# Long convolution and MLP on one core: three channel groups, k loaded without PE transposes, a spectral table built on chip, and listed priorities

## The chip, the cores and the metric

The kernel runs on one core of a Trainium2 chip. The core has five engines, each with an instruction stream that it works through in order: PE (matmuls; its weight loads are shown apart as PEld), DVE (vector), ACT (scalar), POOL (GpSimd) and SP (here it only issues transfers). They are tied together by semaphores. The metric is device time in microseconds, lower is better. The kernel before takes 258.33 us (median of 4 runs, 258.3 to 258.42).

## The reference

The sequence length is S = 2048, the width D = 640, the hidden width F = 1728, all in bf16. With `ln` a layer norm without weights:

```
k_shift[s, d] = sum over t of k_pad[s + t, d] * shift_k[d, 3 - t]     # 4 taps, 3 rows of zeros in front
kv            = k_shift * v
y             = causal convolution over s of kv[:, d] with ssm_k[d, :] (by FFT of length 2 * S) + kv * ssm_D
h             = q + ln(q) * y
out           = h + mish(ln(h) @ w1 + b1) @ w2
```

## The kernel before, in words

The convolution is an FFT written as matmuls. Position s is split as 16 * t1 + t2 (t1 = 0..127, t2 = 0..15). The 640 channels lie in 5 blocks of 128 (`dc`), each of 32 groups of 4 channels, so that there are 160 such groups (`dg`). The stages, by the names in the code:

- `k1` (L485): PE transposes of the loaded `ssm_k` block, 16 per block, evicted from PSUM in two halves (`k1ev`).
- `s1k` and `s1v` (`stage1`, L428 and L429): the DFT over t1, one matmul pair per `dg`. Eight groups make one PSUM tile of 128x1024 f32, and there are 4 tiles per block; each is evicted by `ev` (L317 on ACT, L319 on DVE).
- `s2k` and `s2v` (`s2_pe`, L457): twiddle and DFT over t2. For each of 128 frequencies f a 128x128 block of the table `G` is the stationary operand, and the `nd` channel groups of one group list are the moving one. The lists are `GRP_DC`: blocks 0 to 2 (`nd` 96) and blocks 3 and 4 (`nd` 64). `s2_chunks` packs frequencies into PSUM tiles: 13 chunks of 10 frequencies (960 elements; the last smaller), and 8 of 16 (1024 elements). `s2k` is evicted by `kpev` into `KP`, `s2v` by `xev` (ACT only) into a ring `xa` of 4 slots.
- `swap` (L583): 20 transfers from SBUF to SBUF copy `KP` with its partition halves exchanged into `KPS`. `KPS` lies where `ssm_k` and part of `k` were.
- `ktpe`, `ktev` (L510): k is loaded with t1 on the partitions (L396), and each of its 5 blocks is transposed by 16 PE transposes and evicted in two halves.
- `ks` (L533): the 4-tap shift as matmuls on 32-row tiles of the array, 76 per block, with a part of transposed k as the stationary operand and diagonal taps as the moving one. `kv` (L544, DVE) multiplies by v.
- `prod` (L659, DVE): for each chunk x times `KP` and x times `KPS`, in place.
- `i1` (L670, L671): inverse DFT over g, evicted by `i1ev` into `zb`. `i2` (L712): the last inverse stage per t2.
- Then for each t2: `lnx` (L719), `wb` (L724), `h` (L728), layer norm (L733, L734, POOL), `dr` (L742), transposes (L749); and the MLP in six units of tokens, `m1` (L768), `mish` (L774), `m2` (L784), residual (L793), output.

The order is not that of the code. Each operation is registered with `OP` or `DMA`: its engines and estimated durations, its dependences, its buffer slots and a number `prio`. `_schedule` (L96) is a list scheduler over these estimates: among the operations that can start within 0.3 us of the earliest one, it takes the lowest `prio`. The instructions are then emitted in order of planned start, so that every engine and the SP queue get a fixed order, and on the chip each waits for the head of its own queue. All transfers but those at the start of ACT's and POOL's streams are on SP's queue, and the planner takes them for one serial resource.

Most SBUF is one arena with offsets given by hand. `zb` takes the place of the `bks` and `bvs` buffers of its group, `w1` that of `G`, `w2` that of `KPS`.

Of the kernel before, what the change touches and what calls it, by code (L numbers as in the profile page):

```python
# [10 lines left out]
ALU = mybir.AluOpType  # L11
# [4 lines left out]
S = 2048  # L16
# [10 lines left out]
GRP_DC = [[0, 1, 2], [3, 4]]  # L27
GRP_DG = [(0, 96), (96, 160)]
# [3 lines left out]
OFF_KN = 40960  # L32
OFF_K = 61440
OFF_G = 81920
OFF_BA = 114688
OFF_BB = 139264
OFF_V = 155648
OFF_KK = 176128
OFF_KT = 184320
OFF_KVB = 192640  # L40
OFF_KVB2 = OFF_KK
OFF_XA = OFF_KT
OFF_END = 204928
# [7 lines left out]
OFF_HC = OFF_KT  # L51
OFF_OB = OFF_KT + 3840

# [39 lines left out]
_SEM = 0.18  # L93

# [102 lines left out]
def _make_tables():  # L197
    bf = ml_dtypes.bfloat16
    t1 = np.arange(128, dtype=np.float64)
    f1 = np.arange(128, dtype=np.float64)  # L200
    t2 = np.arange(16, dtype=np.float64)
    g = np.arange(16, dtype=np.float64)
    T = {}
    phi = 2 * np.pi * (f1[None, :] + 0.5) * t1[:, None] / 256
    fcfs = np.stack([np.cos(phi), -np.sin(phi)], axis=1).reshape(128, 256)
    psi = 2 * np.pi * (f1[None, :, None] + 0.5 + 256 * g[None, None, :]) * t2[:, None, None] / 4096
    c, s = np.cos(psi), np.sin(psi)
    R0 = np.zeros((2, 16, 128, 2, 16))
    R0[0, :, :, 0, :] = c
    R0[1, :, :, 0, :] = s  # L210
    R0[0, :, :, 1, :] = -s
    R0[1, :, :, 1, :] = c
    G = np.zeros((2, 2, 16, 2, 128, 2, 4, 16))
    for dp in range(2):
        for dm in range(2):
            G[:, dp, :, dm, :, :, 2 * dp + dm, :] = R0
    T["G"] = G.reshape(128, 128 * 128).astype(np.float32).astype(bf)
    th = 2 * np.pi * g[:, None] * t2[None, :] / 16
    cg, sg = np.cos(th), np.sin(th)
    A1 = np.zeros((2, 4, 16, 2, 16, 4))  # L220
    A2 = np.zeros((2, 4, 16, 2, 16, 4))
    for dl in range(4):
        A1[0, dl, :, 0, :, dl] = cg
        A1[1, dl, :, 0, :, dl] = -cg
        A1[0, dl, :, 1, :, dl] = sg
        A1[1, dl, :, 1, :, dl] = -sg
        A2[0, dl, :, 0, :, dl] = -sg
        A2[1, dl, :, 0, :, dl] = -sg
        A2[0, dl, :, 1, :, dl] = cg
        A2[1, dl, :, 1, :, dl] = cg  # L230
    theta = 2 * np.pi * (f1[:, None, None] + 0.5) * (16 * t1[None, None, :] + t2[None, :, None]) / 4096
    T["t2m"] = np.stack([np.cos(theta) / 2048, -np.sin(theta) / 2048], axis=2).reshape(128, 4096).astype(np.float32).astype(bf)
    consts = np.concatenate([np.eye(128), fcfs, np.tile(np.eye(32), (4, 1)), A1.reshape(128, 128), A2.reshape(128, 128)], axis=1)
    T["consts"] = consts.astype(np.float32).astype(bf)
    return T
# [3 lines left out]
def kernel(  # L239
# [88 lines left out]
    a12_b = consts[:, 416:672].rearrange("p (a f) -> p a f", a=2)  # L328
    mhalf = small.tile([P, 16], F32, name="mhalf")
# [28 lines left out]
    OP("d_consts", ("act", 0.8), w=["consts", "Drow"], emit=emit_consts, prio=-2, lat=3.0)  # L358
# [26 lines left out]

    kn_t = lambda: big("kn", [P, NDC, S], OFF_KN)
    for dc in range(NDC):
        DMA(f"d_kn{dc}", 524e3, (lambda e, dc=dc: nc.sync.dma_start(kn_t()[:, dc, :], A_ssm_k[dc * P:(dc + 1) * P, :])),
            w=[("kn", dc)], prio=1 + dc * 0.01)
    G_t = lambda: big("G", [P, P, P], OFF_G)  # L390
    k_t = lambda: big("k", [P, 16, D], OFF_K)
    v_t = lambda: big("v", [P, 16, D], OFF_V)
    kview = A_k.rearrange("b (p a) d -> p (b a) d", a=16)
    vview = A_v.rearrange("b (p a) d -> p (b a) d", a=16)
    for h in range(2):
        DMA(f"d_k{h}", 1.31e6, (lambda e, h=h: nc.sync.dma_start(k_t()[:, h * 8:(h + 1) * 8, :], kview[:, h * 8:(h + 1) * 8, :])),  # L396
            w=[("k", h)], prio=1.1 + 0.01 * h)
    for c in range(4):
        DMA(f"d_G{c}", 1.05e6, (lambda e, c=c: nc.sync.dma_start(G_t()[:, c * 32:(c + 1) * 32, :].rearrange("p f q -> p (f q)"),
                                                                dram["G"][:, c * 4096:(c + 1) * 4096])),  # L400
            w=[("G", c)], prio=1.2 + 0.01 * c)
# [8 lines left out]
    R_KT = ring("kt", 2)  # L410
# [7 lines left out]
    def stage1(prefix, dc, get_src, src_rt, bname, get_dst, dg_base, prio):  # L418
        for gi in range(4):
# [10 lines left out]
            OP(f"{prefix}pe{dc}_{gi}", ("pe", 0.44), r=["consts"], allocs=[rt], uses=[src_rt], emit=pe, prio=prio,  # L430
# [14 lines left out]
    def s2_pe(prefix, grp, ci, get_src, bname, prio, xa=None, after=()):  # L445
# [4 lines left out]
        def pe(e):  # L450
# [4 lines left out]
            for fl in range(nf):  # L455
# [4 lines left out]
               r=keys + [("G", c) for c in range(f0 // 32, (f0 + nf - 1) // 32 + 1)],  # L460
# [3 lines left out]
    def ps2_views(rt, nd, per, nf):  # L464
        if nf <= per:
            return [(rt.tile[:, 0:nf * nd].rearrange("p (f g) -> p g f", f=nf), 0, nf)]
        if nf == 2 * per:
            return [(rt.tile.rearrange("p (b x) -> p b x", b=2)[:, :, 0:per * nd].rearrange("p b (f g) -> p g b f", f=per), 0, nf)]
        return None

    B_t = [lambda n: big(n + "A", [P, P, 96], OFF_BA), lambda n: big(n + "B", [P, P, 64], OFF_BB)]
# [3 lines left out]
    def kernel_dc(dc, grp):  # L475
# [10 lines left out]
        o1 = OP(f"k1pe{dc}", ("pe", 1.0), r=[("kn", dc), "consts"], allocs=[rt, kk], emit=pe, prio=10)  # L486
# [12 lines left out]
    KT = {}  # L499

    def shift_t(dc, prio):
        rt = _RT(PS, f"kt_{dc}")
        kt = _RT(R_KT, f"kt{dc}")

        def pe(e):
            slot(R_KT, kt, "kT", [P, 16, P + 2], OFF_KT, 4160)
            nc.gpsimd.memset(kt.tile[:, :, 0:2], 0.0)
            pt = ps_alloc(rt, BF16).rearrange("p (t d) -> p t d", t=16)
            for t2 in range(16):
                nc.tensor.transpose(pt[:, t2, :], k_t()[:, t2, dc * P:(dc + 1) * P], ident_b)  # L510
        o1 = OP(f"ktpe{dc}", ("pe", 0.95), r=[("k", 0), ("k", 1), "consts"], allocs=[rt, kt], emit=pe, prio=prio)
        wr = []
        for h in range(2):
            def evf(e, h=h):
                ev(e, kt.tile[:, h * 8:(h + 1) * 8, 2:P + 2], rt.tile.rearrange("p (t d) -> p t d", t=16)[:, h * 8:(h + 1) * 8])
            wr.append(OP(f"ktev{dc}_{h}", EV2(1024), uses=[rt, kt], emit=evf,
                         prio=prio, after=[o1] + wr))
        KT[dc] = (kt, wr)

    def shift_s(dc, prio):  # L520
        kt, wr = KT[dc]
# [3 lines left out]
        def ks(e):  # L525
            kvb.tile = view([P, 64, 16, 2], OFF_KVB + dc * 4096 if dc < 3 else OFF_KVB2 + (dc - 3) * 4096)
            outs = [ps_alloc(x).rearrange("p (i t d) -> p i t d", i=2, t=16) for x in rts]
            for src in range(-3, 16):
                j0, j1 = max(0, -src), min(4, 16 - src)
                for i in range(4):  # L530
                    rows = slice(32 * i, 32 * i + 32)
                    lhs = kt.tile[rows, src, 2:P + 2] if src >= 0 else kt.tile[rows, src + 16, 1:P + 1]
                    nc.tensor.matmul(outs[i // 2][:, i % 2, src + j0:src + j1, :], lhs, diagm[rows, dc * 4 + j0:dc * 4 + j1, :],  # L533
                                     start=(src == -3), stop=(src == 15), skip_group_check=True)
        o2 = OP(f"kspe{dc}", ("pe", 1.3), r=["diagm"], allocs=rts + [kvb], uses=[kt], emit=ks, prio=prio,
                after=wr + ([o for o in ops if o.name.startswith("s1kpe")] if dc >= 3 else []))
# [13 lines left out]
    for grp in range(2):  # L550
        for dc in GRP_DC[grp]:
            kernel_dc(dc, grp)
    for dc in range(NDC):
        shift_t(dc, 10.5 + 0.01 * dc)
    for dc in range(NDC):
        shift_s(dc, 11.5 + 0.01 * dc)
    for grp in range(2):
        nd, per, ch = s2_chunks(grp)
        for ci in range(len(ch)):
# [16 lines left out]
            OP(f"kpev{grp}_{ci}", EV(nf * nd), w=[("KP", grp, ci)], uses=[rt], emit=evf, prio=11, after=[o])  # L576
    def swap(grp):
        nd, per, ch = s2_chunks(grp)
        for half in range(2):
            for g0 in range(GRP_DG[grp][0], GRP_DG[grp][1], 16):  # L580
# [4 lines left out]
                free = ("k1pe",) + (("ktpe",) if g0 >= 80 else ())  # L585
# [4 lines left out]
    swap(0)  # L590
    GRP_BVS = {}
    for grp in range(2):
# [9 lines left out]
    swap(1)  # L602
# [26 lines left out]
    zb_t = [lambda: big("zbA", [P, 2, 16, 384], OFF_BA), lambda: big("zbB", [P, 2, 16, 256], OFF_BB)]  # L629

    for grp in range(2):
# [3 lines left out]
        for ci in range(len(ch)):  # L635
            xa = _RT(R_XA, f"xa{grp}_{ci}")
            free = [x for x in ops if x.name.startswith("kspe")] if ci == 0 else []
# [17 lines left out]
            def f2(e, xa=xa, f0=f0, nf=nf, nd=nd, d0=d0, d1=d1):  # L655
                x = xa.tile[:, 0:nf * nd].rearrange("p (g f) -> p g f", f=nf)
                for tt in (KP_t(), KPS_t()):
                    kp = tt[:, d0:d1, f0:f0 + nf]
# [43 lines left out]
    for t2 in range(16):  # L702
# [5 lines left out]
        def pe(e, t2=t2, rt=rt):  # L708
            py = ps_alloc(rt)
            for grp, (c0, n) in enumerate(((0, 384), (512, 256))):  # L710
                for ri in range(2):
                    nc.tensor.matmul(py[:, c0:c0 + n], t2m_t()[:, t2, ri, :], zb_t[grp]()[:, ri, t2, :], start=(ri == 0), stop=(ri == 1))  # L712
        o_pe = OP(f"i2pe{t2}", ("pe", 0.57), r=["t2m"] + [("zb", 0, gi) for gi in range(12)] + [("zb", 1, gi) for gi in range(8)],
                  allocs=[rt], emit=pe, prio=pr)
# [7 lines left out]
        def wbf(e, rt=rt, lnx=lnx):  # L722
            for (c0, n, d0) in ((0, 384, 0), (512, 256, 384)):
                nc.vector.tensor_tensor(lnx.tile[:, d0:d0 + n], rt.tile[:, c0:c0 + n], lnx.tile[:, d0:d0 + n], ALU.mult)  # L724
# [74 lines left out]

    order = _schedule(ops)  # L800
# [38 lines left out]
```

## Time and profile before

| what | value |
|---|---|
| median of 4 runs | 258.33 us (258.3 to 258.42) |
| the profiled execution | 258.35 us |
| its span, first to last instruction | 256.5 us |
| what lies around the span | 1.85 us |
| PE busy | 227.2 us (89%) |
| DVE busy | 151.2 us (59%) |
| ACT busy | 143.5 us (56%) |
| mean granted PE clock | 0.953 |
| HBM read, written | 20.33 MB, 2.62 MB |

"Busy" is the time in which an engine's instructions run. A row of the profile names line, engine, operation, what is written and read, the shape and the count. "Idle before" is the time for which an engine had nothing running before an instruction, with the instruction that ended the wait. A duration in a row is that of one instruction; neighbours overlap, so where a sum needs the pace of an engine, the distance from start to start in the timeline is used.

### The profile page before, as it was taken

How to read it: one execution, taken by the hardware profiler on the slowest of the kernel's cores; microseconds unless marked ns; L12 is line 12 of the kernel's file. 1: busy time of each engine (PE TensorE's matmuls, PEld its weight loads, DVE VectorE, ACT ScalarE, POOL GpSimd, SP SyncE). 2: the span in 40 equal slices, each digit the busy share in tenths (PEclk: the TensorE clock that was granted, in tenths of full speed). 3: DMA queues.
4: the chain of work that ended last, by engine and by line, in shares of the span. 5: the costliest groups of instructions: out<-in, count | busy, mean ns of one | idle time of the engine just before them, and what ended most of it. 6: DMA issues, size and time to landing. Idle time of an engine off the chain costs nothing.

```text
span 256.5 us, 6925 instructions
## 1 busy us (share of the span) xinstructions
PE 227.2 (89%) x3039; PEld 171.3 (67%) x3039; DVE 151.2 (59%) x297; ACT 143.5 (56%) x196; POOL 22.6 (9%) x56
## 2 busy tenths in 40 slices
PE   8798779848957899849899999999999999999993
PEld 4797778738846799829878746645776467644772
DVE  0778789983799988089798898609912002200121
ACT  2687876616978699957958654565211630066100
POOL 5000000000000000212221223102200000000000
PEclk9999999997995599986999999999999999999999
DMA  6999925999960277300000000000011001000001
GB/s 237 328 419 417 421 100 128 223 221 216 352 270 3 46 301 220 130 0 1 3 0 29 27 3 0 34 20 1 9 45 51 0 3 51 27 28 0 26 28 51
DMA packets 8913, 28.65 MB, mean 112 GB/s; under 512 B 1009, under 2 KB 4914, under 8 KB 7474
## 3 DMA queue, kind: packets, MB, share of 16 engines
q1 hardware_dynamic: 8624, 28.02, 33.0%
q8 instruction: 24, 0.39, 0.6%
q10 hardware_dynamic: 146, 0.17, 0.4%
q0 software_dynamic: 112, 0.01, 0.1%
q14 instruction: 7, 0.06, 0.1%
HBM read 20.33 MB, written 2.62 MB: 90 GB/s over the span
## 4 chain that ended last, share of the span: by engine, by line
PE 64%; DVE 18%; ACT 8%; issue 5%; DMA 3%; SPq 0%; DVEq 0%; ACTq 0%
PE banks L784 24%; PE banks L768 22%; DVE arena L319 6%; DVE arena L659 6%; ACT arena L317 5%; PE banks L428 3%; DMA arena<-in_A_ssm_k_dram 3%; PE banks L671 3%; PE banks L670 2%; DVE arena L544 2%; PE banks L457 2%; PE banks L749 2%; ACT arena L719 2%; PE banks L533 1%; ACT arena L774 1%
## 5 line engine op out<-in xcount | busy, mean ns | idle before, releaser
L317 ACT CAST arena<-banks 128x1024 bf16<-128x1024 f32 (+2 forms) x77 | 72.0, 1008 | 21.1 <-PE banks L429 13.1
L774 ACT ACTIVATE arena<-banks,b1s 128x512 bf16<-128x512 f32 (+2 forms) x84 | 44.3, 545 | 45.1 <-PE banks L768 44.0
L768 PE MATMUL banks<-arena 128*128 128x512 bf16 (+2 forms) x420 | 65.9, 317 | 1.4 <-ACT arena L317 0.8
L784 PE MATMUL banks<-arena 128*128 128x320 bf16 x448 | 62.3, 299 | 0.0
L784 PEld LDWEIGHTS <-arena 128*128 128x128 bf16 x448 | 43.7, 98 | 17.5
L768 PEld LDWEIGHTS <-arena 128*128 128x128 bf16 x420 | 37.5, 103 | 25.3 <-issue 1.7
L793 DVE TENSOR_TENSOR arena<-banks,arena 128x640 bf16<-128x640 f32 x16 | 13.1, 817 | 60.2 <-PE banks L784 60.1
L319 DVE CAST arena<-banks 128x1024 bf16<-128x1024 f32 (+3 forms) x27 | 30.4, 1161 | 10.9 <-PE banks L429 7.1
L457 PE MATMUL banks<-arena 128*128 128x96 bf16 (+1 forms) x512 | 25.0, 210 | 6.8 <-ACT arena L317 3.7
L428 PE MATMUL banks<-consts,arena 128*64 128x128 bf16 x320 | 23.0, 229 | 7.2 <-issue 3.6
L457 PEld LDWEIGHTS <-arena 128*128 128x128 bf16 x512 | 22.7, 105 | 8.8 <-issue 8.3
L317 ACT COPY arena<-banks 128x640 bf16<-128x640 bf16 (+1 forms) x17 | 13.5, 806 | 25.6 <-PE banks L749 18.7
L659 DVE TENSOR_TENSOR arena<-arena 128x960 bf16<-128x960 bf16 (+2 forms) x42 | 24.5, 666 | 0.8 <-ACT arena L317 0.8
L429 PE MATMUL banks<-consts,arena 128*64 128x128 bf16 x320 | 23.4, 230 | 0.0
L429 PEld LDWEIGHTS <-arena 128*64 128x64 bf16 x320 | 20.1, 116 | 4.9 <-issue 4.8
L428 PEld LDWEIGHTS <-arena 128*64 128x64 bf16 x320 | 20.4, 116 | 4.4 <-issue 3.8
L670 PE MATMUL banks<-consts,arena 128*128 128x128 bf16 x160 | 20.1, 228 | 2.3 <-DVE arena L659 2.1
L724 DVE TENSOR_TENSOR arena<-banks,arena 128x384 bf16<-128x384 f32 (+1 forms) x32 | 13.7, 471 | 12.4 <-PE banks L712 7.3
L671 PE MATMUL banks<-consts,arena 128*128 128x128 bf16 x160 | 20.0, 228 | 0.2 <-DVE arena L659 0.2
L670 PEld LDWEIGHTS <-arena 128*128 128x128 bf16 x160 | 16.4, 102 | 2.2 <-DVE arena L659 2.2
L671 PEld LDWEIGHTS <-arena 128*128 128x128 bf16 x160 | 16.4, 103 | 0.8 <-DVE arena L659 0.4
L719 ACT ACTIVATE arena<-arena,nmr,r1v 128x640 bf16<-128x640 bf16 x16 | 14.1, 926 | 1.1 <-DVE arena L728 1.1
(46 smaller groups left out, 168.2 us busy)
## 6 DMA issues: line engine op xcount, KB each, us to landing
arena<-arena SPq DMA_DIRECT2D x20, 256.0 KB, 6.2
arena<-tab_G SPq DMA_DIRECT2D x4, 1024.0 KB, 20.6
arena<-in_A_ssm_k_dram SPq DMA_DIRECT2D x5, 512.0 KB, 6.4
arena<-in_A_k_dram SPq DMA_DIRECT2D x2, 1280.0 KB, 13.8
arena<-in_A_v_dram SPq DMA_DIRECT2D x2, 1280.0 KB, 22.9
arena<-in_A_q_dram SPq DMA_DIRECT2D x2, 1280.0 KB, 9.1
out_dram<-arena SPq DMA_DIRECT2D x16, 160.0 KB, 1.8
arena<-in_B_w_dram SPq DMA_DIRECT2D x1, 2160.0 KB, 8.2
```

Source lines behind the costliest of these rows:

```text
L317: nc.scalar.copy(o, i)
L319: nc.vector.tensor_copy(o, i)
L428: nc.tensor.matmul(ps1[0:64, gl, :], lhs, fcfs_b[:, 0, :], start=True, stop=True)
L429: nc.tensor.matmul(ps1[64:128, gl, :], lhs, fcfs_b[:, 1, :], start=True, stop=True)
L457: nc.tensor.matmul(ps2[:, c0:c0 + nd], G_t()[:, f0 + fl, :], src[:, f0 + fl, :], start=True, stop=True)
L659: nc.vector.tensor_tensor(kp, x, kp, ALU.mult)
L670: nc.tensor.matmul(pz[:, gl, :], KP_t()[:, dg, :], a12_b[:, 0, :], start=True, stop=False)
L671: nc.tensor.matmul(pz[:, gl, :], KPS_t()[:, dg, :], a12_b[:, 1, :], start=False, stop=True)
L719: nc.scalar.activation(lnx.tile, xn_t()[:, t2, :], ACT.Identity, scale=r1v[:, t2:t2 + 1], bias=nmr1[:, t2:t2 + 1])
L768: nc.tensor.matmul(ph[:, 0:w], w1_t()[:, dc, fc * P:(fc + 1) * P], lnhT_t()[:, dc, c0:c0 + w], start=(dc == 0), stop=(dc == NDC - 1))
L774: nc.scalar.activation(ub_t[u % 2]()[:, fc, 0:w], rt.tile[:, 0:w], ACT.Mish, bias=b1s[:, fc:fc + 1], scale=1.0)
L784: nc.tensor.matmul(po[:, hf2 * 512:hf2 * 512 + 320], hb[:, fc, tl * P:(tl + 1) * P], w2_t()[:, fc, hf2 * 320:(hf2 + 1) * 320], start=(fc = ...
```

## The change

1. Three groups instead of two: blocks 0 and 1, blocks 2 and 3, block 4 (`nd` 64, 64, 32). A pass of `s2` has 3 x 128 matmuls instead of 2 x 128, and 8 + 8 + 4 = 20 chunks of 1024 elements instead of 21. The buffers between `s1` and `s2` and `zb` follow the groups; `i2` has three column ranges (6 matmuls instead of 4) side by side in its PSUM tile, and `wb` reads all 640 columns in one instruction instead of two.
2. `k` is loaded by 5 transfers straight into the layout of the shift, channel block on the partitions and 2048 positions along them, behind 16 zeros written once by POOL. `ktpe` and `ktev` are gone. The stationary operand of `ks` is now read with a step of 16 elements (32 bytes). The rows that these transfers read are runs of 2048 consecutive elements of k as it is stored, 640 of them; they are not the 640 columns of k.
3. `G` (4 MB in 4 transfers) is no longer loaded. Its nonzero part `R` (1 MB, one transfer) and a 128x4 `mask` (on ACT's queue) are, and 16 DVE `tensor_scalar` instructions (`gb`), each of 1024 elements per partition, fill `G`. `R` lies in the place of the ring `xa`, whose first use waits for the `gb`. `xa` no longer shares its place with transposed k.
4. Before planning, the `prio` of 55 stages is replaced by the number in the table `PRIO`. Planned durations of `k1pe`, `s1` and `d_consts` go up a little.
5. `swap` waits, for the part of `KPS` that lies over `k`, for the `ks` of the blocks that it covers.

The core of the diff:

```diff
-GRP_DC = [[0, 1, 2], [3, 4]]
-GRP_DG = [(0, 96), (96, 160)]
+GRP_DC = [[0, 1], [2, 3], [4]]
+GRP_DG = [(32 * g[0], 32 * g[-1] + 32) for g in GRP_DC]
+NGRP = len(GRP_DC)
+KTP = 16 + S
+PRIO = {
+    "ks2": -46.0, "s2k2": -45.99, "prod1": -43.96, "kv2": -38.99, "s2v1": -35.75, "s1k1": -33.38, "s2k0": -17.03, "s1v4": -0.1,
+    "d_swap2": 1.04, "prod0": 2.94, "kv4": 3.02, "d_kn0": 3.04, "kv0": 3.04, "d_kn4": 3.06, "d_kn3": 3.45, "d_kn2": 4.97, "gb2": 4.97,
+    "kv3": 4.97, "s1k2": 4.98, "i11": 5.56, "ks1": 5.58, "s1k4": 5.89, "d_kn1": 6.14, "d_R": 6.4, "d_v1": 6.6, "prod2": 6.77,
+    "s1k0": 6.78, "k11": 7.61, "gb0": 8.54, "ks4": 9.51, "d_kT0": 10.73, "i12": 11.16, "gb3": 11.17, "d_kT1": 12.39, "k10": 12.41,
+    "s2k1": 13.35, "c_diag": 14.62, "d_v0": 16.46, "s1k3": 17.64, "k13": 17.91, "s1v1": 18.01, "d_kT3": 20.42, "ks3": 21.0, "k14": 23.67,
+    "s1v3": 23.77, "d_kT4": 24.6, "s2v0": 25.75, "s1v0": 26.06, "d_kT2": 26.64, "gb1": 26.93, "kv1": 26.93, "s1v2": 26.95, "ks0": 27.94,
+    "d_swap1": 37.95, "s2v2": 39.7, "k12": 39.9, "i10": 40.61, "d_swap0": 42.48,
+}
...
+        nc.scalar.dma_start(mask[:], dram["mask"])
-    OP("d_consts", ("act", 0.8), w=["consts", "Drow"], emit=emit_consts, prio=-2, lat=3.0)
+    OP("d_consts", ("act", 1.2), w=["consts", "Drow", "mask"], emit=emit_consts, prio=-2, lat=3.0)
...
-    for h in range(2):
-        DMA(f"d_k{h}", 1.31e6, (lambda e, h=h: nc.sync.dma_start(k_t()[:, h * 8:(h + 1) * 8, :], kview[:, h * 8:(h + 1) * 8, :])),
-            w=[("k", h)], prio=1.1 + 0.01 * h)
+    DMA("d_R", 1.05e6, lambda e: nc.sync.dma_start(R_t().rearrange("p f q -> p (f q)"), dram["R"]), w=["R"], prio=1.015)
+    OP("kTpad", ("pool", 0.2), w=["kTpad"], emit=lambda e: nc.gpsimd.memset(kT_t()[:, :, 0:16], 0.0), prio=0)
+    for dc in range(NDC):
+        DMA(f"d_kT{dc}", 1.05e6, (lambda e, dc=dc: nc.sync.dma_start(kT_t()[:, dc, 16:KTP], A_k.rearrange("b s d -> (b s d)").rearrange("(c p x) -> c p x", c=5, p=P)[dc])),
+            w=[("kT", dc)], prio=1.1 + 0.01 * dc)
     for c in range(4):
-        DMA(f"d_G{c}", 1.05e6, (lambda e, c=c: nc.sync.dma_start(G_t()[:, c * 32:(c + 1) * 32, :].rearrange("p f q -> p (f q)"),
-                                                                dram["G"][:, c * 4096:(c + 1) * 4096])),
-            w=[("G", c)], prio=1.2 + 0.01 * c)
+        for dl in range(4):
+            def gb(e, c=c, dl=dl):
+                dst = G_t()[:, c * 32:(c + 1) * 32, :].rearrange("p f (r d g) -> p (f r) d g", r=2, d=4)[:, :, dl, :]
+                src = R_t()[:, c * 32:(c + 1) * 32, :].rearrange("p f (r g) -> p (f r) g", r=2)
+                nc.vector.tensor_scalar(dst, src, mask[:, dl:dl + 1], None, ALU.mult)
+            OP(f"gb{c}_{dl}", ("dve", 0.36), r=["R", "mask"], w=[("G", c, dl)], emit=gb, prio=8 + c)
...
-    def shift_t(dc, prio):
-        rt = _RT(PS, f"kt_{dc}")
...
-                    lhs = kt.tile[rows, src, 2:P + 2] if src >= 0 else kt.tile[rows, src + 16, 1:P + 1]
+                    lhs = kT_t()[rows, dc, 16 + src:16 + src + 16 * (P - 1) + 1:16]
...
-                free = ("k1pe",) + (("ktpe",) if g0 >= 80 else ())
+                free = ("k1pe",) + tuple(f"kspe{c}" for c in range(NDC) if c * KTP * 2 < (g0 - 64) * 256 and (g0 - 80) * 256 < KT_END(c))
...
-            for grp, (c0, n) in enumerate(((0, 384), (512, 256))):
+            for grp, (d0, d1) in enumerate(GRP_DG):
                 for ri in range(2):
-                    nc.tensor.matmul(py[:, c0:c0 + n], t2m_t()[:, t2, ri, :], zb_t[grp]()[:, ri, t2, :], start=(ri == 0), stop=(ri == 1))
+                    nc.tensor.matmul(py[:, 4 * d0:4 * d1], t2m_t()[:, t2, ri, :], zb_t[grp]()[:, ri, t2, :], start=(ri == 0), stop=(ri == 1),
+                                     skip_group_check=True)
...
-            for (c0, n, d0) in ((0, 384, 0), (512, 256, 384)):
-                nc.vector.tensor_tensor(lnx.tile[:, d0:d0 + n], rt.tile[:, c0:c0 + n], lnx.tile[:, d0:d0 + n], ALU.mult)
+            nc.vector.tensor_tensor(lnx.tile, rt.tile[:, 0:D], lnx.tile, ALU.mult)
...
+    for o in ops:
+        o.prio = PRIO.get(_stage(o.name), o.prio)
     order = _schedule(ops)
```

`_stage` maps an operation's name to its stage and first number (`s2kpe2_1` and its eviction `kpev2_1` to `s2k2`, `xev0_3` to `s2v0`). The first number is the channel block for `k1`, `s1`, `ks`, `kv` and the loads, the group for `s2`, `prod`, `i1` and `d_swap`, and the quarter of the table for `gb`. What the table does not name keeps its `prio`: the q loads 3, `t2m` 3.1, `w1` and `w2` 4, and everything from `i2` on.

## The prediction

> **What bounds the kernel now.** I read the page's 40 slices first. The PE row is full from slice 18 to the end: the MLP is bound by PE. Before that no row is full for long, and the full one changes.
>
> ```profile
> PE   8798779848957899849899999999999999999993
> DVE  0778789983799988089798898609912002200121
> ACT  2687876616978699957958654565211630066100
> PEclk9999999997995599986999999999999999999999
> ```
>
> So I cut the span where the work changes and asked for the busy time of each engine in each stage (columns: window, its length, then busy us and instructions of PE, PEld, DVE, ACT, POOL, granted PE clock, DMA share, GB/s).
>
> ```profile
> core 0: us, PE busy (x) PEld busy (x) DVE busy (x) ACT busy (x) POOL busy (x), PEclk, DMA share, GB/s
> 5.00:25.00 20.00, 17.46 (x426) 16.28 (x426) 14.38 (x23) 14.31 (x15) 0.00 (x0) 1.00 1.02 387
> 25.00:39.00 14.00, 11.17 (x273) 10.48 (x271) 11.55 (x12) 11.03 (x13) 0.00 (x0) 1.00 0.63 259
> 39.00:58.00 19.00, 13.60 (x544) 11.58 (x543) 17.22 (x27) 8.73 (x10) 0.38 (x3) 1.00 0.90 196
> 58.00:70.00 12.00, 10.92 (x264) 10.25 (x265) 6.80 (x6) 10.11 (x11) 0.00 (x0) 0.86 1.03 277
> 70.00:95.50 25.50, 19.09 (x309) 17.53 (x307) 24.69 (x44) 20.24 (x23) 0.36 (x1) 0.73 0.44 166
> 95.50:107.60 12.10, 12.10 (x218) 12.00 (x215) 6.43 (x15) 11.90 (x14) 1.92 (x3) 1.00 0.58 186
> 107.60:118.30 10.70, 6.24 (x49) 4.76 (x48) 8.40 (x22) 6.66 (x11) 1.59 (x4) 0.79 0.00 1
> 118.30:256.50 138.20, 132.84 (x966) 87.16 (x964) 61.41 (x151) 59.05 (x102) 14.82 (x34) 0.99 0.06 20
> ```
>
> From 118.3 us on PE runs 132.84 of 138.20 us, and the change leaves that work as it is. What can move is the front, 5 to 107.6 us. There DVE is busy 14.38 + 11.55 + 17.22 + 6.80 + 24.69 + 6.43 = 81.1 us and ACT 76.3 us of 102.6: 157.4 of 205.2 us, so 47.8 us are idle, 23.9 per engine. From 39 to 58 us DVE is full and ACT lacks 10.3; from 70 to 95.5 DVE is full again; from 95.5 on ACT is full and DVE lacks 5.7. The front waits on whichever of the two is full, while the other stands still. DVE's timeline shows why (start, length):
>
> ```profile
> 40.23 1.29 DVE L544 TENSOR_TENSOR arena<-banks,arena 128x512 bf16<-128x512 f32 x2 [0.30 <-PE banks L533]
> ...
> 61.73 1.23 DVE L319 CAST arena<-banks 128x1024 bf16<-128x1024 f32 x1 [4.12 <-PE banks L429]
> ...
> 70.18 20.70 DVE L659 TENSOR_TENSOR arena<-arena 128x960 bf16<-128x960 bf16 x36
> ```
>
> The reader is to see three phases one after another: `kv` from 40 us, a gap of 4.12 us while s1v's matmuls start over, then 36 `prod` in a row, with nothing to share. SP's queue has the swaps ahead of the loads of q:
>
> ```profile
> 40.01 22.76 SPq L583 DMA_DIRECT2D arena<-arena  x20
> 62.86 1.33 SPq L607 DMA_DIRECT2D arena<-in_A_q_dram  x2
> ```
>
> **The change, part by part.** The sum is made against the profiled execution, 258.35 us = span 256.5 + 1.85 around it; the median of 258.33 is the same within 0.02. Spacings below are start to start in the timeline.
>
> ```profile
> L319 DVE COPY arena<-banks 128x1024 bf16<-128x1024 bf16 x14 | 9.1, 684 | 1.0 <-PE banks L485 0.8
> L742 DVE TENSOR_SCALAR arena<-arena,mv,r 128x640 bf16<-128x640 bf16 x16 | 7.1, 441 | 0.6 <-POOL r L346 0.6
> L533 PEld LDWEIGHTS <-arena 32*128 32x128 bf16 x380 | 5.4, 93 | 2.7 <-issue 2.1
> ```
>
> *Evictions of transposed k go.* 10 of 1024 elements, 5 on ACT (spacing 0.91) and 5 on DVE (0.60): −7.6 us of eviction time.
>
> *`gb`, 16 on DVE, comes.* The near row is L742: 441 ns, 0.37 spacing, 640 elements, two scalar columns. The Trainium skill, "VectorE: DVE Perf Modes", section "The perf-mode tier table", puts a bf16 `tensor_scalar` within SBUF at four elements a cycle; 640 elements would then need 167 ns beside the some 158 ns that remain of L728's 491 at two a cycle, 325 in all, and the row shows 441. The rule alone gives about 0.37 spacing for 1024 elements, 5.9 us; the row plus 384 elements at the rule's slope gives 0.47; the copy L319 at two a cycle has 0.60, with a scalar column perhaps 0.66, 10.6 us. I take 0.50, near L742: 16 x 0.50 = 8.0 us, range 5.9 to 10.6. The destination is written in runs of 16 elements; `k1ev` writes runs of 2 and is in the 684 ns row, so I exclude slower. They lie on DVE ahead of s2k; their cover is DVE's 5.6 us of idle time in 5 to 25 us. Without cover they cost 8.0.
>
> *Chunks.* 42 evictions of s2 (21 a pass) and 42 `prod` instructions become 40 and 40 of 1024 elements. For prod 24 x 0.57 + 2 x 0.47 + 16 x 0.60 = 24.2 becomes 24.0; the evictions come out equal. Sum on DVE and ACT: −7.6 + 8.0 − 0.2 = +0.2, +0.1 us per engine (−1.0 to +1.4).
>
> *PE.* 80 transposes at 56 ns go: −4.5. In s2 the spacing is 42 ns for 96 columns and 29 for 64; a pass was 128 x 0.042 + 128 x 0.029 = 9.1. No row has 32 columns. By the two rows (0.42 per column + some 2) it would be 16 ns; the Trainium skill, "TensorE: Matmul & The Clock Gate", section "Wait — 56ns, not 53.3ns?", says that starts never come closer than about 25 ns. This speaks against a group of 32. With 16 ns a pass is 9.5 (+0.8 for both), with 25 it is 256 x 0.029 + 128 x 0.025 = 10.6 (+3.0), with 29 it is +4.1. I take the rule's +3.0. The weights of `ks` are read with steps of 32 bytes: L485, strided, runs at 64 ns, L510, dense, at 56. L533's four loads of a set start 3 ns apart and last 93 ns each, thus side by side; 95 sets x 8 ns = +0.8. One after another they would cost 380 x 64 ns = 24 us, which that overlap excludes. Sum on PE −0.7, range −3.7 to +1.2, hidden: PE idles 18.3 us in the front. Without that cover it would count in full.
>
> *Transfers.* G's 4 MB become 1 MB: −3.1 MB at 411 GB/s (10 to 20 us), 7.6 us, so v is there at about 27 instead of 35.4. On its own it earns nothing: the first `kv` came at 40.23, behind s2k in PE's queue. 5 loads of k replace 2 (three more issues of about 0.5 us on SP, and one for R against four for G). That k is read as other runs of the same bytes has no bearing on the time. The mask is one more issue on ACT (L357's took 0.62), covered by ACT's idle 4 us before 7.24. POOL's five small memsets become one.
>
> *`wb`.* 0.85 us in the chain (L724 x2) becomes one like L793, 817 ns, some 0.75 spacing: −0.1 for each of the two token tiles that start the MLP, −0.2. `i2` keeps its 1280 columns per tile: 32 more matmuls x 2.5 ns, nothing.
>
> *The order.* By work alone the result would be 258.35 + 0.1 − 0.2 = 258.25. The rest is idle time. Three groups and the new priorities let `kv` run beside s2k's evictions, let group 2's `prod` begin after 4 swaps instead of 12, and put `i1` of one group beside `prod` of the next. I choose, stage by stage, what is left of 23.9 us per engine: 5 to 25 us 5.6 to 3.5 (gb fills it), s2k 2.7 to 2.0, kv 6.0 to 2.5, s1v 3.5 to 2.0, prod 3.0 to 2.0, end 2.9 to 1.5: 13.5 left, −10.4. This is a choice; its ends are 0 and −23.9. What is late next is PE: about 73 us of work in the front at full clock.
>
> Forecast: 258.35 + 0.1 − 0.2 − 10.4 = **247.8 us**.
>
> **Rivals.** *(A) is the forecast.* *(B) The floor comes near:* 6.5 us idle per engine, as in slices with both at 8 to 9: 258.25 − 17.4 = 240.8. For it: nothing in the data flow needs the three phases; against: before i1 the swaps, 20 x 1.14 = 22.8 us in one queue, still wait for s2k and now for `ks` too. *(C) All that goes was hidden and the order gives nothing:* 258.3. For it: the work sum; against: ACT's 10.3 us of idleness beside a full DVE. *(D) Slower: the q loads stand ahead of the swaps.* They keep `prio` 3, swaps of groups 1 and 0 get 38 and 42. On SP's queue a q load that waits for the last `kv` holds 16 swaps behind it. Before, `kv` ended at 57.6. Then q and t2m (3.6 MB, 9 us), 16 swaps (18 us) and 4 us to land give 88.6; 16 prods (9.6 us) and the way from the last prod to the first `i2` (95.5 to 107.4, 11.9 us) give 110.1 instead of 107.4: +2.7, 261.0. It decides from a last `kv` at about 55 us on. For it: `ks0` and `kv1` have late numbers; against: `kv` no longer waits for transposes of k.
>
> **How the numbers follow.** A 0.53, own range 241 to 255; B 0.12; C 0.10, of which 0.03 within 0.2% (half a microsecond, about what a measurement of this kernel can tell from no change), 0.05 faster, 0.02 slower; D 0.25. Faster 0.53 + 0.12 + 0.05 = 0.70, same 0.03, slower 0.02 + 0.25 = 0.27. The range takes in A and C, most of B's spread and half of D's, whose wait has no upper bound in the trace: 239 to 262. The bounds of gb and PE (1.4 us) lie within.
>
> **What would show it.** Right: `gb` at 0.45 to 0.75 us each; starts 25 ns apart in s2's 32-column chunks; idle time of DVE and ACT in the front near 13.5 each; first `kv` before 35 us, first `prod` before 60, first `i2` at about 97. Wrong: SP waiting long at a q load with swaps behind (D); PE at half clock through the front, so that its 73 us become the bound; a `gb` above 1 us.

## The result, and the profile after

The changed kernel takes 248.03 us (median of 11 runs, 246.37 to 249.37) beside 258.3 us (16 runs): a ratio of 0.9605, 95% interval 0.9575 to 0.9635, or 10.2 us less. A few executions of a kernel take over 1.5% longer than its fastest one; the ratios leave them out. The forecast was 247.8. The profiled execution took 248.29 us, with a span of 246.4.

The slices of the changed kernel, in the rows shown of before:

```profile
PE   7597998699699998499999999999999999999993
DVE  0479799689999994896888996159511011200121
ACT  2478875599899999569588537554104610166000
PEclk9979999799999999959999999999999999999999
```

The front ends nearly two slices earlier, and DVE and ACT are now high in the same slices, above all from slice 12 to 15, where before one was full while the other stood low. The MLP behind is as it was. The stages, in the columns used before; the cut at 97.0 is where `i2` begins (96.86, before 107.44):

```profile
core 0: us, PE busy (x) PEld busy (x) DVE busy (x) ACT busy (x) POOL busy (x), PEclk, DMA share, GB/s
5.00:25.00 20.00, 15.40 (x363) 14.14 (x364) 13.99 (x28) 12.56 (x13) 0.00 (x0) 0.91 1.02 382
25.00:39.00 14.00, 13.08 (x464) 12.29 (x461) 12.86 (x18) 11.74 (x13) 0.00 (x0) 1.00 0.13 48
39.00:58.00 19.00, 16.05 (x524) 14.90 (x519) 15.28 (x18) 13.40 (x15) 0.00 (x0) 0.91 0.67 148
58.00:70.00 12.00, 9.41 (x316) 8.61 (x316) 11.59 (x19) 10.65 (x12) 0.00 (x0) 1.00 0.91 206
70.00:95.50 25.50, 24.45 (x528) 23.55 (x525) 25.17 (x44) 25.06 (x29) 0.47 (x2) 1.00 0.77 288
95.50:97.00 1.50, 1.50 (x30) 1.49 (x28) 0.16 (x1) 1.50 (x2) 1.36 (x3) 1.00 1.05 364
```

From 5 to 97 us DVE is busy 79.05 us and ACT 74.91 of 92, so they idle 12.95 and 17.09, 15.0 per engine, where it was 23.9. Their work is 154.0 us instead of 157.4, 1.7 less per engine. Idle −8.9 and work −1.7 make −10.6, which is how far `i2` moved. From 70 to 95.5 us hardly any idle time is left on either: both are busy over 25.0 of 25.5 us. From the first `i2` to the end it was 149.06 us and is 149.54.

DVE's timeline (start, length) and the rows of the new or reshaped instructions:

```profile
16.57 4.83 DVE L429 TENSOR_SCALAR arena<-arena,mask 128x1024 bf16<-128x1024 bf16 x12
...
31.56 2.48 DVE L543 TENSOR_TENSOR arena<-banks,arena 128x512 bf16<-128x512 f32 x4
...
59.70 6.10 DVE L659 TENSOR_TENSOR arena<-arena 128x1024 bf16<-128x1024 bf16 x10
```

```profile
L485 PE MATMUL banks<-arena 128*128 128x32 bf16 x256 | 7.6, 176 | 1.5 <-DVE arena L429 0.9 <-ACT arena L339 0.5
...
L532 PEld LDWEIGHTS <-arena 32*128 32x128 bf16 x380 | 6.9, 147 | 1.7 <-issue 1.4
L429 DVE TENSOR_SCALAR arena<-arena,mask 128x1024 bf16<-128x1024 bf16 x16 | 6.6, 481 | 0.0
```

`gb` (L429) lasts 481 ns and starts every (4.83 − 0.48) / 11 = 0.395 us. The first `kv` (L543) comes at 31.56 instead of 40.23, and the first ten `prod` (L659) run as one at 59.70, before the last `kv` at 69.84. In the first row a wait is named that was not foreseen: PE waits for `gb`, 0.9 us in all.

### The profile page after: what moved, and what is told of

Its sections match the earlier page's. It is cut to its first block, busy times and chain, and to the rows that moved or that the text cites. A ratio compares the mean times of both kernels' runs of the same rounds, so it can differ in the third digit from the quotient of the medians.

```text
span 246.4 us, 7340 instructions
## 1 busy us (share of the span) xinstructions
PE 223.4 (91%) x3247; PEld 170.5 (69%) x3247; DVE 148.2 (60%) x283; ACT 142.1 (58%) x194; POOL 22.2 (9%) x52
## 4 chain that ended last, share of the span: by engine, by line
PE 67%; ACT 12%; DVE 12%; issue 4%; DMA 3%; SPq 0%; ACTq 0%; DVEq 0%
PE banks L783 25%; PE banks L767 23%; ACT arena L339 9%; PE banks L485 5%; DMA arena<-in_A_ssm_k_dram 3%; PE banks L456 3%; DVE arena L543 3%; PE banks L670 3%; PE banks L457 2%; DVE arena L429 2%; PE banks L671 2%; PE banks L748 2%; ACT arena L719 2%; DVE arena L341 2%; DVE arena L723 2%
## 5 line engine op out<-in xcount | busy, mean ns | idle before, releaser
L339 ACT CAST arena<-banks 128x1024 bf16<-128x1024 f32 x76 | 71.6, 1043 | 13.3 <-PE banks L485 6.4
L792 DVE TENSOR_TENSOR arena<-banks,arena 128x640 bf16<-128x640 f32 x16 | 13.1, 818 | 60.4 <-PE banks L783 60.4
L341 DVE CAST arena<-banks 128x1024 bf16<-128x1024 f32 x24 | 28.3, 1220 | 6.1 <-PE banks L457 5.1
L485 PE MATMUL banks<-arena 128*128 128x64 bf16 (+1 forms) x768 | 25.5, 187 | 5.7 <-DVE arena L543 2.3
L456 PE MATMUL banks<-consts,arena 128*64 128x128 bf16 x320 | 23.5, 234 | 4.1 <-DVE arena L341 2.4
L339 ACT COPY arena<-banks 128x640 bf16<-128x640 bf16 (+1 forms) x16 | 12.5, 796 | 23.4 <-PE banks L748 18.1
L659 DVE TENSOR_TENSOR arena<-arena 128x1024 bf16<-128x1024 bf16 x40 | 24.4, 688 | 0.4 <-ACT arena L339 0.4
L457 PEld LDWEIGHTS <-arena 128*64 128x64 bf16 x320 | 20.9, 120 | 5.0 <-issue 4.8
L457 PE MATMUL banks<-consts,arena 128*64 128x128 bf16 x320 | 23.7, 236 | 0.0
L456 PEld LDWEIGHTS <-arena 128*64 128x64 bf16 x320 | 21.2, 120 | 0.5
L670 PE MATMUL banks<-consts,arena 128*128 128x128 bf16 x160 | 18.9, 219 | 0.5 <-ACT arena L339 0.5
L671 PE MATMUL banks<-consts,arena 128*128 128x128 bf16 x160 | 18.8, 219 | 0.0
L723 DVE TENSOR_TENSOR arena<-banks,arena 128x640 bf16<-128x640 f32 x16 | 12.7, 794 | 9.6 <-PE banks L712 7.5
```

What stands on the lines that cost most here:

```text
L339: nc.scalar.copy(o, i)
L341: nc.vector.tensor_copy(o, i)
L456: nc.tensor.matmul(ps1[0:64, gl, :], lhs, fcfs_b[:, 0, :], start=True, stop=True)
L457: nc.tensor.matmul(ps1[64:128, gl, :], lhs, fcfs_b[:, 1, :], start=True, stop=True)
L485: nc.tensor.matmul(ps2[:, c0:c0 + nd], G_t()[:, f0 + fl, :], src[:, f0 + fl, :], start=True, stop=True)
L659: nc.vector.tensor_tensor(kp, x, kp, ALU.mult)
```

## The experiments

"Order kept" means that the changed kernel's (or the old kernel's) sequence of operations is emitted unchanged and only the instructions of one operation differ. Where it does not say so, the planner made a new sequence. The kernels with the five direct loads of k read it as the changed kernel does, as runs of stored elements; those with k transposed use its columns. The column us is the median of all executions. The ratio is to the kernel before on the same chip, and a gain or loss below is, unless said otherwise, the difference of two ratios times 258.3 us.

| kernel | us | ratio, 95% interval |
|---|---|---|
| old order kept, no transposes of k | 254.74 | 0.983 [0.9795, 0.9866] |
| before + k loaded, planned anew | 265.96 | 1.0329 [1.0291, 1.0367] |
| parts 2 and 3, two groups, old priorities | 255.29 | 0.9865 [0.981, 0.9921] |
| the change without `PRIO` | 252.62 | 0.9733 [0.9649, 0.9817] |
| the change, table loaded, planned anew | 279.68 | 1.0817 [1.0736, 1.0898] |
| the change, table loaded, order kept | 251.7 | 0.9713 [0.9676, 0.9749] |
| the change, `gb` twice, order kept | 256.48 | 0.9855 [0.9757, 0.9952] |
| the change, k transposed, planned anew | 272.6 | 1.0591 [1.0549, 1.0633] |
| the same instructions, another plan | 273.48 | 1.0627 [1.0562, 1.0693] |
| k transposed, priorities of its own | 250.9 | 0.9705 [0.964, 0.9769] |
| the change + filler matmuls | 245.81 | 0.9529 [0.9488, 0.957] |
| k transposed, own priorities, filler | 248.09 | 0.9616 [0.9566, 0.9666] |

### Without the priority table

```diff
-    for o in ops:
-        o.prio = PRIO.get(_stage(o.name), o.prio)
```

> The changed kernel without its table of priorities: three groups, direct load of k and the built table stay, every stage has the priority of the kernel before. Theory 'order' (the gain is idle time that the listed priorities take away): most of it goes, 254 to 258 us, and kv, s1v and prod stand one after another again, with 20 us or more idle per engine up to the first i2. Theory 'groups' (three groups suffice, whatever the priorities): 248 to 251. Theory 'work' (the removed transposes and evictions pay): 248 to 250.

The three groups and the new instructions under the old priorities already win 6.9 us by the ratio; the table wins the other 3.3. The ratio rests on two executions, 249.03 and 252.19 us, so the table's share is anything from 1 to 5.6 us. The time lies near the ranges of 'groups' and 'work', which it does not separate, and away from that of 'order'.

### Two groups, old priorities

```diff
-GRP_DC = [[0, 1], [2, 3], [4]]
+GRP_DC = [[0, 1, 2], [3, 4]]
...
-    for o in ops:
-        o.prio = PRIO.get(_stage(o.name), o.prio)
```

`i2` and `wb` go back to two column ranges with it.

> Two groups as before, with the direct load of k, the built table, and the old priorities; against the run with three groups and the old priorities (252.6 us) it shows what the third group does when the planner orders by the same numbers. Theory 'order' (three groups are what lets prod and i1 start early): 256 to 260. If the groups matter only with the listed priorities: 251 to 254. The rows of k read are those of the changed kernel.

255.29 us, −3.5, between the two ranges expected. With the run before it this makes a ladder: the new k load and built table −3.5, the third group a further −3.4, the priorities a further −3.3. The last two steps are known only within some 1 to 6 us each, and each step is also a new sequence, so the ladder says that all three help and does not price them.

### Only k's load, and only the table's load: both planned anew

```diff
-    for h in range(2):
-        DMA(f"d_k{h}", 1.31e6, ...)
+    for dc in range(NDC):
+        DMA(f"d_kT{dc}", 1.05e6, ..., w=[("kT", dc)], prio=1.1 + 0.001 * dc)
```

> The kernel before with part 2 of the change alone: k by five direct loads, no PE transposes and no evictions of them, two groups, table loaded, old priorities. The rows read are 2048 consecutive stored elements, as in the changed kernel, so the shift sees other data than in the kernel before. Theory 'order': the 7.6 us of evictions and 4.5 us of transposes lay in stages with idle time, 256.5 to 258.5. Theory 'work': half of 7.6 us per engine at the least, 254.5 or below.

265.96 us: slower, against both theories. The planner made another sequence. DVE's timeline of that kernel (L523 is `kv`):

```profile
35.79 3.68 DVE L523 TENSOR_TENSOR arena<-banks,arena 128x512 bf16<-128x512 f32 x6 [10.06 <-DMA arena<-in_A_v_dram]
```

`kv` now stands ahead of most evictions of s2k, and v, queued behind the loads of k and of the table, lands at 35.67. DVE does nothing for 10 us.

```diff
-            OP(f"gb{c}_{dl}", ("dve", 0.36), r=["R", "mask"], w=[("G", c, dl)], emit=gb, prio=8 + c)
+        DMA(f"d_G{c}", 1.05e6, ..., w=[("G", c, dl) for dl in range(4)], prio=6.4 + 0.01 * c)
```

> The changed kernel with the whole 4 MB table loaded in four transfers in the place of the 1 MB transfer, and without the sixteen gb. If gb's 6.3 us on DVE are hidden by idle time (as forecast) and the transfer is what was worth removing: 3.1 MB more at 411 GB/s make k and v 7.6 us late, 250 to 255. If gb is on the path and the transfers are hidden: 243 to 247. If both are hidden: 247.5 to 248.5.

279.68 us, also outside what was expected. SP's queue has the q loads and `t2m` (70.6 to 72.9 us) ahead of the last four swaps, which land only at 87.7 to 90.7; in the changed kernel the last swap lands at 71.4. Neither run says what its part costs: each measured a sequence. So the next ones keep the sequence.

### No transposes of k, the old order kept

```diff
-                nc.tensor.transpose(pt[:, t2, :], k_t()[:, t2, dc * P:(dc + 1) * P], ident_b)
...
-                ev(e, kt.tile[:, h * 8:(h + 1) * 8, 2:P + 2], rt.tile.rearrange("p (t d) -> p t d", t=16)[:, h * 8:(h + 1) * 8])
+                pass
```

The kernel before with `ktpe` and `ktev` left out; the shift works on zeros.

> The kernel before with its own planned order kept, in which the 80 PE transposes of k and their ten evictions are simply not issued; the slots that they would fill are zeroed once by POOL at the start, so the shift works on zeros. It prices the removed work alone, with no new plan. By the forecast's term (7.6 us of evictions and 4.5 us on PE, in stages with idle time): 255.5 to 258.3 us. By theory 'work' (they lie on the path): 4 us or more off, 254.5 or below.

254.74 us, −4.4 (−5.3 to −3.5). Work that leaves PE, DVE and ACT is worth its time even in the old order. This speaks against the idea that the idle time of the front would take it up. In the profiled execution, 3.3 us shorter than that of the kernel before, the first `i2` starts 2.5 us earlier (104.91 us); the rest lies behind it, where nothing was removed.

### The table loaded, the new order kept

```diff
-                nc.vector.tensor_scalar(dst, src, mask[:, dl:dl + 1], None, ALU.mult)
+                pass
...
+            nc.sync.dma_start(G_t()[:, c * 32:(c + 1) * 32, :].rearrange("p f q -> p (f q)"), dram["G"][:, c * 4096:(c + 1) * 4096])
```

`gb` is left out, and the 4 MB are loaded in the place of `R`.

> The changed kernel with its own planned order kept; where it loads the 1 MB table it loads the whole 4 MB, and the sixteen gb are not issued. It prices gb against the transfer without a new plan. If the 3 MB more (7.6 us of transfer ahead of v and k) are on the path: 250 to 256 us. If gb's 6.3 us on DVE are on the path and the transfer is hidden: 242 to 247. The forecast had both hidden: 247 to 249.

251.7 us, 2.8 (1.6 to 4.0) more than the changed kernel: in this order, building the table beats loading it. PE's and DVE's timelines show what gates s2k instead of `gb`, and the first `kv` (L492 is the matmul of s2k, L539 that of `ks`, L550 `kv`):

```profile
20.61 1.89 PE L492 MATMUL banks<-arena 128*128 128x32 bf16 x64 [3.83 <-DMA arena<-tab_G]
23.43 1.03 PE L492 MATMUL banks<-arena 128*128 128x32 bf16 x32
...
35.97 2.49 DVE L550 TENSOR_TENSOR arena<-banks,arena 128x512 bf16<-128x512 f32 x4 [1.39 <-PE banks L539]
```

The kept order reads the third quarter of the table first (`gb2` has the lowest number of the four). It lands at 20.57, though the first two have landed at 14.37 and 18.07. So the first three chunks of s2k start at 20.61, some 21.5 and 23.43 instead of 18.29, 19.87 and 21.45. PE, having waited, is granted 0.50 of its clock from 20 to 25 us, where the changed kernel has 1.00. The first `kv` comes at 35.97 instead of 31.56. It is not v that it waits for: v has landed at 26.27 and 31.80 (19.03 and 24.65 in the changed kernel), and what ends the wait is `ks` on PE, behind s2k. A load that brings the third quarter first was not tried; part of the 2.8 us may belong to this order of the four transfers.

### `gb` twice

```diff
                 nc.vector.tensor_scalar(dst, src, mask[:, dl:dl + 1], None, ALU.mult)
+                nc.vector.tensor_scalar(dst, src, mask[:, dl:dl + 1], None, ALU.mult)
```

> The changed kernel with each gb issued twice, 6.3 us more on DVE at the same places of the same order. The forecast says that gb lies in idle time of DVE between 5 and 25 us: +0 to +2 us, 248 to 250. If DVE is the path there: +5 to +6.5 us, 253 to 254.5.

256.48 us, 6.5 more than the changed kernel (some 3.8 to 9.1 by the interval). The first 24 `gb` take 11.0 us until DVE's next other instruction, where the first 12 took 4.7: 0.52 us for each one added, 8.4 us for 16. Most of it is paid. PE's timeline shows where, first in the changed kernel:

```profile
18.29 0.96 PE L485 MATMUL banks<-arena 128*128 128x32 bf16 x32
19.87 0.96 PE L485 MATMUL banks<-arena 128*128 128x32 bf16 x32 [0.62 <-DVE arena L429]
21.45 0.96 PE L485 MATMUL banks<-arena 128*128 128x32 bf16 x32
```

and with each `gb` twice (L486 is the same matmul):

```profile
18.84 0.96 PE L486 MATMUL banks<-arena 128*128 128x32 bf16 x32 [2.02 <-DVE arena L430]
22.51 1.03 PE L486 MATMUL banks<-arena 128*128 128x32 bf16 x32 [2.71 <-DVE arena L430]
26.18 1.04 PE L486 MATMUL banks<-arena 128*128 128x32 bf16 x32 [1.64 <-DVE arena L430]
```

One chunk needs one quarter of the table, which is four `gb`. The chunks start 1.58 us apart, which is 4 x 0.395, and 3.67 apart when there are eight. `gb` sets the pace of s2k's first chunks. Over all chunks of 32 columns PE now waits for `gb` 8.0 us instead of 0.9:

```profile
L486 PE MATMUL banks<-arena 128*128 128x32 bf16 x256 | 7.8, 181 | 8.5 <-DVE arena L430 8.0 <-ACT arena L339 0.5
```

A second loss comes with it: from 20 to 30 us PE is granted 0.55 and then 0.50 of its clock, where it had 1.00. The two lines are the columns of the stage table, for the doubled kernel:

```profile
20.00:25.00 5.00, 2.03 (x48) 1.75 (x48) 4.79 (x12) 2.27 (x3) 0.00 (x0) 0.55 1.01 413
25.00:30.00 5.00, 3.81 (x86) 3.78 (x88) 4.40 (x7) 1.64 (x3) 0.00 (x0) 0.50 0.32 123
```

So the 6.5 us are the price of later chunks and of a slower PE together; the run does not part them.

### The same instructions in another order

```diff
-        DMA(f"d_kT{dc}", 1.05e6, ...
+        DMA(f"d_kT{dc}", 524e3, ...
```

Only the planned size of k's loads is changed (to the true one); the planner then finds another sequence of the same instructions.

> The changed kernel, every instruction of it, with one planned number altered: the planner is told 524 KB instead of 1.05 MB for each of the five loads of k (each moves 512 KB). The planner then orders otherwise, and two swaps of the last group come behind the q loads and t2m on SP's queue. It prices the order alone, at equal work. Theory 'order' (and rival D of the prediction, q loads ahead of swaps): 262 to 270 us, with the first i2 at about 115. Theory 'work': 246 to 250, since nothing is added or removed.

273.48 us: some 25 us by order alone, more than was expected. SP's timeline of that kernel (L583 swaps, L607 q):

```profile
34.53 32.42 SPq L583 DMA_DIRECT2D arena<-arena  x18
68.33 0.83 SPq L607 DMA_DIRECT2D arena<-in_A_q_dram  x2
71.34 0.33 SPq L610 DMA_DIRECT2D arena<-tab_t2m  x1
71.71 1.29 SPq L583 DMA_DIRECT2D arena<-arena  x2
```

and its chain:

```profile
72.40 11.90 DMA arena<-arena
84.52 9.73 DVE arena L659 x16
```

Two swaps behind q and `t2m` are enough: the last one takes 11.9 us to land where the swaps of the changed kernel take 5.2 in the median, and the products wait for it until 84.5. A further 8.4 us are lost before the last ten products, which begin at 106.27 because the evictions of s2v that they read are late. PE, waiting too, is granted 0.51 of its clock from 86 to 100 us. `i2` starts at 123.0 instead of 96.9.

### k transposed again, and with priorities of its own

```diff
-    DMA(f"d_kT{dc}", 1.05e6, ...)
+    DMA(f"d_k{h}", 1.31e6, ...)
...
+                nc.tensor.transpose(pt[:, t2, :], k_t()[:, t2, dc * P:(dc + 1) * P], ident_b)
...
+                ev(e, tile_()[:, h * 8:(h + 1) * 8, 2:P + 2], ...)
```

The columns of k are transposed as before, all else is the change.

> The changed kernel with part 2 undone: k is loaded with time on the partitions, its 640 columns are transposed by 80 PE transposes and evicted, as in the kernel before, so the shift works on the columns of k again; groups, built table and priorities stay. s2k of the first two groups waits for the transposes, since raw k lies in its output's place. Theory 'order': +1 to +4 us (half of 7.6 us of evictions per engine, part of it hidden), 249 to 252. Theory 'work': 253 to 256.

272.6 us, a miss: `PRIO` was kept, and for this set of operations the planner put q and `t2m` (69.3 to 72.6) ahead of the last four swaps, which land at 85.8 to 87.7. That is the delay of the run above once more, so the transposes were not what it measured. With priorities searched for this kernel by the planned end alone:

```diff
-PRIO = {"ks2": -46.0, "s2k2": -45.99, ...}
+PRIO = {"c_diag": 12.9528, "d_kn0": -20.3933, ...}
```

> The run with k's columns transposed on PE again (272.6 us), with priorities of its own found by a random search over the planner's own planned end; swaps stand ahead of the q loads. If the 272.6 came from an order that did not fit: 250 to 254 us. If the transposes and evictions themselves cost it: 260 or more.

250.9 us, with all swaps ahead of q: some 22 us less than the same instructions under the other kernel's table. It is 2.6 us behind the changed kernel, with intervals that nearly meet: three groups, the built table and a fitting order keep most of the gain while k's own columns are used.

### Filler in PE's wait

In the changed kernel the clock falls to half at 103.6 us, just when the MLP begins. The stretch 103.6 to 110.4 in the columns of the stage table:

```profile
103.60:110.40 6.80, 6.02 (x59) 5.94 (x57) 6.59 (x19) 4.60 (x11) 1.22 (x4) 0.50 0.01 4
```

```diff
+        if t2 == 2:
+            def fill(e):
+                pf = ps_alloc(frt)
+                for i in range(6):
+                    nc.tensor.matmul(pf[:, 0:512], warm[:, 0:128], warm[:], start=True, stop=True)
+            OP("fill", ("pe", 1.3), allocs=[frt], emit=fill, prio=81.1, after=[o_pe])
```

> The changed kernel with six more matmuls of 512 columns on zeros (1.3 us), issued on PE after the i2 of the third token tile, where PE waits for the chain from i2 to the first MLP matmul. In the profile the granted clock is half from 103.6 to 110.4 us, and the first 70 MLP matmuls start 105 ns apart instead of 56. If idle PE time lowers the clock: no half clock there and 1 to 3 us less, 245 to 247. If the clock falls anyway, or ACT's mish sets the pace: 248.

245.81 us, better than both kernels; its interval ends just below that of the changed kernel. PE's timelines of the changed kernel

```profile
102.33 0.71 PE L712 MATMUL banks<-arena 128*128 128x256 bf16 x6 [1.68 <-DVE arena L723]
...
104.45 2.83 PE L767 MATMUL banks<-arena 128*128 128x128 bf16 x25 [0.78 <-ACT arena L339]
```

and with the filler (L721; L775 is the same MLP matmul)

```profile
100.52 1.46 PE L721 MATMUL banks<-warm 128*128 128x512 bf16 x6
102.35 0.71 PE L712 MATMUL banks<-arena 128*128 128x256 bf16 x6 [0.38 <-DVE arena L731]
...
104.47 1.56 PE L775 MATMUL banks<-arena 128*128 128x128 bf16 x25 [0.78 <-ACT arena L339]
```

The 1.68 us wait became 0.38; the chain starts at the same time and takes 1.56 us instead of 2.83, the next 45 matmuls 2.78 instead of 4.02. That is 2.5 us, about what the time shows (2.0 by the ratios). The stretch then has

```profile
103.60:110.40 6.80, 6.02 (x103) 5.82 (x101) 6.59 (x19) 5.73 (x19) 1.20 (x4) 1.00 0.01 4
```

full clock, and 103 matmuls instead of 59. The same filler in the kernel with k transposed and its own priorities:

> The kernel that transposes k's real columns on PE, in its own found order (250.9 us), plus six matmuls of zeros right after i2 of the third token tile, in PE's wait before the MLP. In the trace of that kernel the clock stands at half from about 108 to 110.4 us, when the first MLP chain runs (25 matmuls in 2.82 us against 1.56 with the filler in the changed kernel). Theory, an idle PE lowers the clock for the work that comes next: the half-clock stretch goes, about 1.3 us are won, 249 to 250 us. Rival, the gain of the filler in the changed kernel was another order of the MLP's start: nothing here, 250.5 to 251.5 us.

248.09 us, 2.3 less by the ratios; the two intervals meet. Its clock is full from 99 to 115 us, and the first MLP chain takes 1.56 us, not 2.82. The two profiled executions are 1.9 us apart: the chain accounts for 1.3, and `i2` starts 0.6 us earlier (99.70 instead of 100.29), though the filler comes only later. In the front the granted clock was 0.50 from 18.5 to 21.9 us without the filler and 1.00 with it, so the 0.6 look like the clock of that one execution and not like the filler's doing. This version transposes k's columns and is as fast as the changed kernel without filler.

## Why the prediction was right, and where it was not

The total was right within 0.2 us, and that closeness is luck: the idle term was a choice between 0 and −23.9, and the errors of the terms cancel. The work fell by 1.7 us per engine where +0.1 was forecast, 1.8 us better than put; idle time fell by 8.9 where 10.4 was put, 1.5 worse; and from the first `i2` to the end the kernel takes 0.5 us more where 0.2 less was forecast, 0.7 worse. The mechanism, idle time that a better order takes out of the front, held: 8.9 of the 10.6 us in the front are idle time, and the same instructions in two orders are some 25 us apart. How much of it is due to the priorities and how much to the groups is known only roughly.

- **"Their cover is DVE's 5.6 us of idle time in 5 to 25 us": failed.** DVE idles 6.01 us there after (20 − 13.99), and nearly all of it lies where `gb` cannot go. The changed kernel's stage in the columns of the stage table, cut where the first `gb` starts (`R` has landed at 14.8):

```profile
5.00:16.57 11.57, 8.62 (x172) 7.87 (x172) 5.68 (x13) 5.71 (x6) 0.00 (x0) 0.85 1.03 362
16.57:25.00 8.43, 6.78 (x194) 6.27 (x194) 8.31 (x17) 6.85 (x8) 0.00 (x0) 1.00 1.01 409
```

  From 16.57 us on DVE idles 0.12 us; before the change it idled 2.00 in the same stretch, and 12 `gb` need 4.7. The slip was to count idle time in a stage as free, without asking when the new work can start and what waits for it: a chunk of s2k waits for its four `gb`. Doubled, they cost 6.5 us of the 8.4 added. What the first 16 cost was not measured, and PE's 0.9 us of waiting for them beside 8.0 speaks for less. In the sum `gb` counted +4.0, half of 8.0 as a load shared by two engines; at the measured 0.395 us they are 6.3 us of work.
- **Transfers, "on its own it earns nothing": failed in part.** That the first `kv` stands behind s2k in PE's queue is true of the new order too, and no run shows that v's earlier landing earns anything. What the term left out is that s2k waits for the table itself: with the table loaded, its first chunk waits 3.83 us for a transfer and starts 2.3 us later, the first `kv` 4.4 us later, and the time is 2.8 more although DVE has 16 instructions less.
- **Evictions of k, −7.6 over two engines, −3.8: held.** Alone, in the old order, −4.4 (−5.3 to −3.5), PE's transposes included. "By work alone the result would be 258.25" did not hold: the work on DVE and ACT fell by 1.7 us per engine where +0.1 was forecast. `gb`'s finer pace explains (8.0 − 6.3) / 2 = 0.85 of that; the rest was not isolated.
- **Idle, −10.4 to 13.5 per engine, "a choice": −8.9, to 15.0.** The stage that missed most is the first, 3.5 chosen and (6.01 + 7.44) / 2 = 6.7 found, again the cover; then 39 to 58 us, 2.5 chosen and (3.72 + 5.60) / 2 = 4.7 found. The last stages came out better than chosen: 0.4 us in 70 to 95.5 where 2.0 were left.
- **PE: held, with the rule's value.** 32 matmuls of 32 columns take 0.96 us: (0.96 − 0.176) / 31 = 25 ns from start to start. The two rows of before would have given 16; the 25 ns that the Trainium skill states ("TensorE: Matmul & The Clock Gate", section "Wait — 56ns, not 53.3ns?"), the rule that spoke against the change, is what the trace shows, and without it the step would have been +0.8 instead of +3.0. The strided weight loads take 147 ns instead of 93. A block of `ks`, two of before (the second line has 74 of its block's 76 matmuls) and one of after:

```profile
38.92 1.27 PE L533 MATMUL banks<-diagm,arena 32*128 32x32 bf16 x76
46.89 1.08 PE L533 MATMUL banks<-diagm,arena 32*128 32x32 bf16 x74
...
29.99 1.36 PE L532 MATMUL banks<-diagm,arena 32*128 32x32 bf16 x76
```

  That is 0.1 to 0.3 us more, or 0.5 to 1.4 for five blocks, around the +0.8 that was put. For `gb` the rule alone gave 0.37, nearer to 0.395 than the 0.50 chosen by the row.
- **`wb`, −0.2: a little too much.** In the second and third token tile the next instruction starts 0.81 us after its one instruction, where with two it started 0.88 and 0.87 after the first: −0.13 for both.
- **Rival (D), q ahead of the swaps: did not occur here, but is real.** The changed kernel's q load waits 4.6 us for the last `kv` with no swap behind it. In three replanned kernels q stood ahead of two or four swaps, and they took 273 to 280 us: the price put on it, 261.0, was too low. It was the plan, not the priorities 38 and 42 read one by one, that decided.
- **(B) and (C)** are excluded by the time; (C) also by the ladder.

## What to carry to other kernels

Idle time on an engine covers new work only where nothing waits for that work: ask when it can start, and for its consumer, first. In a planned kernel every edit, even an estimate's, makes a new order and can cost ten times what the edit does (the loaded table cost 2.8 us in the kept order and 31 in a new one); to price a part keep the order frozen, and search the priorities again for what is kept. Where an engine under a clock throttle waits ahead of a dense stretch, a few filler matmuls may pay for themselves.

## What the runs showed of the hardware

- A half-idle PE can cost the clock without any long wait: PE is busy 3.08 of 6.60 us from 97 to 103.6 with no single wait above 1.68, and is then granted half for 6.8 us under full load. With the filler it is busy 4.37 of the 6.60 and stays at 1.00. The Trainium skill ("TensorE: Matmul & The Clock Gate", section "Why this matters for your kernels") asks for no idle gaps above some 3 us; here much shorter ones in a row were enough.
- Reading the stationary operand with a step of 32 bytes costs a 32x128 load 147 ns instead of 93, though little of it is seen (0.1 to 0.3 us in a block of 76), since four such loads start within 12 ns and run side by side.
- `gb`, a `tensor_scalar` of 1024 bf16 elements per partition written in runs of 16, lasts 481 ns and starts every 0.395 us.
- A swap of 256 KB issued behind the loads of q and `t2m` took 11.9 us to land instead of 5.2 in the median.
